# An attention and mixer kernel on one core: attention values formed in 64x64 quarters over two PSUM banks, tail transposes moved into another bank and one step later

## The chip, the cores and the metric

The kernel runs on one core of a Trainium2 chip. The metric is the device time of one execution in microseconds; the times below are medians over runs on the chip. A profile is taken of one execution, and all rows in this document come from that execution.

## What is computed

The program is an attention block with a learned relative-position bias, followed by two mixer blocks. The change touches only the attention block:

```
q, k, v: (B=4, H=8, S=576, D=64)
scores = q @ k^T / sqrt(64)
rel    = |i - j|;  x = log1p(rel) / log1p(max(i, 1))
bias   = relu(x * w1 + b1) @ w2                  # one value per head, row, column
attn   = softmax(scores + bias)
out    = attn @ v                                # (4, 8, 576, 64), all float32
...
x = first mixer(out);  result = second mixer(x)
```

576 = 4 x 128 + 64, so each head has four full row tiles of 128 and a tail of 64 rows, and likewise four full blocks of keys and a tail of 64 keys.

## The kernel before, in words

**Units.** Attention is worked through in 80 units. A unit is one batch `b`, one pair of heads `p` and one row tile `it`; `it` = 4 (`NM`) is the tail of 64 rows, whose two heads share one tile. The first 20 units are batch 0, in the order tail, 0, 1, 2, 3, with the four head pairs inside. The next 50 units are ten (batch, head pair) groups of five units in the order 0, 1, tail, 2, 3; these groups are called *paired* here (function `paired`), because the values of two row tiles are formed together. The last 10 units are two groups that are not paired.

**Steps.** The main loop (L656 of the kernel before) runs steps n = -3 to 80. Step n works on several units at once, and what it emits is the order in which each engine does it:

- PE: `scores(n+3)`: queries times keys in 64x64 quarters (`ss`, L456): lhsT is 64 rows x 64 columns of the array, and the four quarters go to two PSUM tiles, one for each half of the array's rows.
- DVE: scale, bias and row minimum (`pr`, L464), then ACT: exp with a row sum (`softmax`, L475), then POOL: division by the sum (`normalise`, L488).
- PE: `turn(n)`: the probabilities of unit n are transposed, 128x128 at a time: four blocks of keys of the first head into the bank `x` (L515), four of the second head into the bank `y` (L520), and the two heads' tail keys into the bank `z` (L521, L523). ACT copies `x` (L516) and `z` (L528, `z_out`) to SBUF, DVE copies `y` (L532, `y_out`).
- PE: `q_turn(n+5)`, in batch 0 alone: a query tile is transposed into the second half of the bank `z` (L412), and ACT copies it out (L423, L425, `q_out`).
- PE: `values`: the transposed probabilities times `v`. `values` (L542 to L547) forms one unit; `values2` (L565 to L570) forms two row tiles of a paired group in two halves, in two steps, the second half with the tail keys. The first head goes to the array's columns 0 to 63 and the second to 64 to 127 (128 rows x 64 columns, two matmuls side by side); the tail keys are 64 rows x 64 columns. All of it is summed in one bank `o`, and DVE copies it into X (`place`, L438, or L552 for the 64-row tail).

**Where the values stand.** `values` and `values2` calls come at a step's end (`late_v`: after transposes and, in batch 0, bias work), but one of each paired group comes early in a step (`early_v`: `values` of the group's tail unit, straight after `scores`). Of the 80 calls, 40 are halves of `values2` and 40 are `values`; 10 of the latter are the paired groups' early ones, and one more early one stands near the end.

**Bias.** The first 15 steps (n = -3 to 11) also make the bias: per step two groups of 16 rows. DVE makes three quarters of the hidden layer and ACT one (`hidden`, L320 and L322), PE multiplies (`bps`, L363; 32 matmul records a step) and ACT copies out (`bias_place`, L376). Steps 0 to 3 are tail units and have no `y`; from step 4 on there is one.

**PSUM.** There are eight banks. Four are `s0` and `s1` (scores and bias products, two banks each), and one each `x`, `y`, `z` and `o`. A tile of such a bank is given out again when the last reader of the tile before has ended; the wait for that stands on the first instruction that writes the new tile. The engines run in the order in which the code emits, and each waits at the head of its own queue.

Float32 matmuls stand in the trace as two records each (two passes), transposes as one.

Of the kernel before, what the change touches and what calls it, by code (L numbers as in the profile page):

```python
# [7 lines left out]
F32 = mybir.dt.float32  # L8
# [3 lines left out]
ALU = mybir.AluOpType  # L12
# [7 lines left out]
def kernel(ctx, tc, ins, consts, out, dbg=None, nb=4, stop=None):  # L20
    nc = tc.nc
    V, S, G, T, D = nc.vector, nc.scalar, nc.gpsimd, nc.tensor, nc.sync

    q, k, v = ins["q"], ins["k"], ins["v"]
    B, H, N, HD = q.shape
    P = 128
    NP = H // 2
    NM = N // P
    TL = N - NM * P
# [9 lines left out]
    ident = cpool.tile([P, P], F32, name="ident")  # L39
    X = cpool.tile([P, ND, NT], F32, name="X")  # L40
# [14 lines left out]
    halves = (slice(0, HD), slice(HD, P))  # L55
# [112 lines left out]
    units = [(0, p, it) for it in order0 for p in range(NP)]  # L168
# [5 lines left out]
    NB = N + TL  # L174
# [4 lines left out]
    bias_t = apool.tile([P, NP, N], F32, name="bias_t")  # L179
    raw_p = tc.alloc_tile_pool(name="raw", bufs=2)  # L180
    hl_p = tc.alloc_tile_pool(name="hl", bufs=2)
    pp = tc.alloc_tile_pool(name="pp", bufs=4)
    pt_p = tc.alloc_tile_pool(name="pt", bufs=1)
    sm_p = tc.alloc_tile_pool(name="sm", bufs=4)

# [221 lines left out]
    def q_turn(n, z):  # L407

        b, p, it = units[n]
        w = P if it < NM else TL  # L410
        if b == 0:
            T.transpose(z[:, 1, 0:w], qraw.pop((b, p, it)), ident[0:w, 0:w])  # L412
        else:
            queries[n] = turned(b, p)[:, it * P:it * P + w]

    def q_out(n, z):
        b, p, it = units[n]
        if b > 0:
            return
        w = P if it < NM else TL  # L420
        t = hl_p.tile([P, P], F32, tag="q0", name="q0", bufs=5)[:, 0:w]
        if it < NM:
            S.copy(out=rows(t), in_=dealt(z[:, 1]))  # L423
        else:
            S.copy(out=t, in_=z[:, 1, 0:w])  # L425
        queries[n] = t


# [1 line left out]
    def dealt(x):  # L430
        return x.rearrange("p (t j s) -> p t s j", j=GT, s=P // GT)

    def rows(x):
        return x.rearrange("p (t s j) -> p t s j", j=GT, s=P // GT)

    def place(p, c0, o):

        V.tensor_copy(  # L438
            out=X[:, p, c0:c0 + o.shape[1]].rearrange("p (t j s) -> p t j s", j=GT, s=P // GT),
            in_=o.rearrange("p (t s j) -> p t j s", j=GT, s=P // GT),  # L440
        )
# [62 lines left out]
    def room(n):  # L504
        if not paired(n):
            return rooms[0], n % 2
        it = units[n][2]
        return (rooms[0], it) if it < 2 else (rooms[1], 1 if it == NM else it - 2)

    def turn(n, pr, z):  # L510
        b, p, it = units[n]
        (xs, ys, zs), s_ = room(n)
# [4 lines left out]
        if it < NM:  # L517
            y = ps_t.tile([P, NM, P], F32, tag="y", name="y")
            for t in range(NM):
                T.transpose(y[:, t], pr[:, NB + t * P:NB + (t + 1) * P], ident)  # L520
            T.transpose(z[:, 0], pr[:, NM * P:N + TL], ident)  # L521
            return ys[:, s_], zs[:, s_], y
        T.transpose(z[0:TL, 0], pr[:, NM * P:N], ident)  # L523
        return None, zs[:, s_], None

    def z_out(z, zs, y):
        r = slice(0, P if y is not None else TL)
        S.copy(out=zs[r], in_=z[r, 0])  # L528
# [5 lines left out]
    def values(n):  # L534
        b, p, it = units[n]
        vm, vt = vraw[b, p]
        (xs, ys, zs), s_ = room(n)
        xs, ys, zs = xs[:, s_], ys[:, s_], zs[:, s_]
        o = ps_t.tile([P, P], F32, tag="o", name="o")
        w = P if it < NM else TL  # L540
        for t in range(NM):
            T.matmul(o[0:HD, 0:w], lhsT=vm[:, t, 0], rhs=xs[:, t, 0:w], start=t == 0, stop=False)  # L542
            rh = ys[:, t] if it < NM else xs[:, t, TL:P]
            T.matmul(o[HD:P, 0:w], lhsT=vm[:, t, 1], rhs=rh, start=t == 0, stop=False)
        T.matmul(o[0:HD, 0:w], lhsT=vt[0:TL, 0], rhs=zs[0:TL, 0:w], start=False, stop=True)
        lh, rh = (vt[TL:P, 1], zs[TL:P]) if it < NM else (vt[0:TL, 1], zs[0:TL, TL:P])
        T.matmul(o[HD:P, 0:w], lhsT=lh, rhs=rh, start=False, stop=True)  # L547
        c0 = b * N + it * P
        if it < NM:
            place(p, c0, o)  # L550
        else:
            V.tensor_copy(out=X[:, p, c0:c0 + w], in_=o[:, 0:w])  # L552

    open_o = []

    def values2(n, half):

        b, p, it = units[n]
        vm, vt = vraw[b, p]
        xs, ys, zs = room(n)[0]  # L560
        if half == 0:
            open_o.append(ps_t.tile([P, 2 * P], F32, tag="o", name="o"))
        o = open_o[0]
        for t in range(2 * half, 2 * half + 2):
# [4 lines left out]
        T.matmul(o[0:HD], lhsT=vt[0:TL, 0], rhs=zs[0:TL], start=False, stop=True)
        T.matmul(o[HD:P], lhsT=vt[TL:P, 1], rhs=zs[TL:P], start=False, stop=True)  # L570
        c0 = b * N + it * P
        place(p, c0, open_o.pop())
# [32 lines left out]
    for gi in range(GUP):  # L605
        if gi == NQ:
            load_q0(order0[1])
        if gi < NP:
            k_parts0(gi, hl_p if gi < 2 else first, "" if gi < 2 else "x")
        if HP and gi > 0:  # L610
            bias_place(groups[gi - 1], bps)
        if gi == TW:
            times_w1(slice(TC, 2 * N))
        if gi >= 1:
            hide(gi + 2)
        if not HP and gi > 0:
            bias_place(groups[gi - 1], bps)
        bps = bias_product(gi, hs.pop(gi))
        if gi >= GUP - 2:
            u = gi - (GUP - 2)  # L620
            z = ps_t.tile([P, 2, P], F32, tag="z", name="z")
            q_turn(u, z)
            q_out(u, z)
    bias_place(groups[GUP - 1], bps)
# [33 lines left out]
    st = {}  # L658
    for n in range(-3, U + 1):
# [7 lines left out]
            normalise(*st[n + 2])  # L667
        if len(gs) > 0:
            hide(gs[0] + 2)
        z = ps_t.tile([P, 2, P], F32, tag="z", name="z") if n < U else None  # L670
        form(early_v.pop(n, []))
        if n == U - 1:
            early_x([NM])
        if 0 <= n < U:
            ys, zs, y = turn(n, st[n][0], z)
        if n == U - 3:

            flat = bias_m.rearrange("p i h n -> p (i h n)").bitcast(F32R)
# [8 lines left out]
        if 0 <= n + 5 < U:  # L687
            q_turn(n + 5, z)
# [3 lines left out]
        if 0 <= n < U:  # L692
            z_out(z, zs, y)
        if 0 <= n + 5 < U:
            q_out(n + 5, z)
# [654 lines left out]
```

## Time and profile before

| what | us |
|---|---|
| median of 3 runs | 914.84 (914.71 to 916.07) |
| the profiled execution, its time | 913.72 |
| its span, first to last instruction | 911.9 |
| PE busy | 894.5 (98%) |
| DVE busy | 625.6 (69%) |
| ACT busy | 394.0 (43%) |
| POOL busy | 293.7 (32%) |
| granted TensorE clock, mean | 0.997 of 2.4 GHz |

Attention takes about the first 340 us. A timeline row gives the start in us from the span's start, the duration in us, engine, line, operation, tiles (out<-in), for PE the array's rows*columns, shapes (partitions x elements) and the number of instructions merged in the row; in square brackets stands how long the engine had been idle and what ended that. PE is its matmuls, PEld its weight loads. Ends of matmuls are modelled, so on PE the starts are what to read.

### The profile page before, as it was taken

How to read it: one execution, taken by the hardware profiler on the slowest of the kernel's cores; microseconds unless marked ns; L12 is line 12 of the kernel's file. 1: busy time of each engine (PE TensorE's matmuls, PEld its weight loads, DVE VectorE, ACT ScalarE, POOL GpSimd, SP SyncE). 2: the span in 40 equal slices, each digit the busy share in tenths (PEclk: the TensorE clock that was granted, in tenths of full speed). 3: DMA queues.
4: the chain of work that ended last, by engine and by line, in shares of the span. 5: the costliest groups of instructions: out<-in, count | busy, mean ns of one | idle time of the engine just before them, and what ended most of it. 6: DMA issues, size and time to landing. Idle time of an engine off the chain costs nothing.

```text
span 911.9 us, 18151 instructions
## 1 busy us (share of the span) xinstructions
PE 894.5 (98%) x7018; PEld 749.8 (82%) x7018; DVE 625.6 (69%) x1371; ACT 394.0 (43%) x875; POOL 293.7 (32%) x430
## 2 busy tenths in 40 slices
PE   8799999999999999999999999999999999999998
PEld 3366776665666789899999999999999989889996
DVE  6799777887877769988834343232215999896756
ACT  6799766676666754433312121211114532222310
POOL 2366455555545532233310100100002452423230
PEclk9999999999999999999999999999999999999999
DMA  8775534333332113223400100000041001010002
GB/s 157 161 155 118 115 64 94 54 66 68 56 64 56 29 60 93 94 93 121 133 24 24 38 33 24 24 24 1 1 77 48 24 1 47 1 59 1 1 13 92
DMA packets 118966, 54.87 MB, mean 60 GB/s; under 512 B 100832, under 2 KB 107616, under 8 KB 118880
## 3 DMA queue, kind: packets, MB, share of 16 engines
q1 hardware_dynamic: 118880, 53.72, 24.7%
q8 instruction: 55, 0.90, 0.4%
q14 instruction: 31, 0.25, 0.1%
HBM read 38.36 MB, written 4.72 MB: 47 GB/s over the span
## 4 chain that ended last, share of the span: by engine, by line
PE 78%; DVE 16%; issue 2%; ACT 2%; DMA 2%; SPq 0%; DVEq 0%; ACTq 0%
PE a L985 14%; PE pg L822 14%; PE ss L456 9%; PE x L515 5%; PE o L565 4%; PE po L1202 4%; PE pv L1096 4%; PE ps L1171 4%; PE o L542 3%; PE y L520 3%; PE bps L363 3%; PE pu L1149 3%; DVE res L940 2%; DVE w L131 2%; PE pu L854 1%
## 5 line engine op out<-in xcount | busy, mean ns | idle before, releaser
L488 POOL TENSOR_SCALAR pr<-pr,sm 128x576 f32<-128x576 f32 (+2 forms) x208 | 129.1, 637 | 118.8 <-DVE sm L482 114.2
L985 PE MATMUL a<-g,c 128*128 128x384 f32 x864 | 162.4, 335 | 1.8 <-DVE X L993 1.0
L985 PEld LDWEIGHTS a<-g,c 128*128 128x128 f32 x864 | 150.9, 188 | 3.5 <-ACT g L828 2.2
L829 DVE SCALAR_TENSOR_TENSOR g<-pg,g 128x384 fp32r<-128x384 f32 x72 | 40.0, 556 | 163.7 <-ACT g L828 163.7
L822 PE MATMUL pg<-u,c 128*128 128x384 f32 x720 | 134.5, 334 | 0.0
L822 PEld LDWEIGHTS pg<-u,c 128*128 128x128 f32 x720 | 125.6, 188 | 0.1
L828 ACT ACTIVATE g<-pg 128x384 fp32r<-128x384 f32 x72 | 35.3, 490 | 192.2 <-PE pg L822 192.2
L475 ACT ACTIVATE pr<-pr,mn 128x576 f32<-128x576 f32 x144 | 112.0, 778 | 6.9 <-DVE mn L464 6.0
L464 DVE CUSTOM_DVE_ANT_0 pr<-ss,bias_m 128x576 f32<-128x576 f32 x128 | 91.3, 750 | 29.8 <-PE ss L456 29.2
L456 PE MATMUL ss<-kt,X 64*64 64x288 f32 x864 | 77.1, 412 | 0.0
L940 DVE STREAM_TRANSPOSE res<-X 32x256 f32<-32x256 f32 (+1 forms) x176 | 68.1, 387 | 2.8
L60 POOL TENSOR_TENSOR c<-w,c 128x512 fp32r<-128x512 f32 x24 | 35.5, 1479 | 88.9 <-ACT c L59 78.7
L60 POOL TENSOR_TENSOR wi<-w,wi 128x512 fp32r<-128x512 f32 x8 | 14.0, 1754 | 153.0 <-DVE g L829 112.5
L320 DVE TENSOR_SCALAR X<-ttab,wsm 128x576 f32<-128x576 f32 x108 | 62.3, 639 | 0.0
L515 PEld LDWEIGHTS x<-ident,pr 128*128 128x128 f32 x320 | 33.6, 141 | 30.4 <-POOL pr L488 18.9
L1171 PE MATMUL ps<-wsT,vn 128*128 128x288 f32 x384 | 56.5, 296 | 1.1 <-DVE tmp L1181 1.1
L456 PEld LDWEIGHTS ss<-kt,X 64*64 64x64 f32 x864 | 36.6, 132 | 22.3 <-DVE sm L482 7.3
L1171 PEld LDWEIGHTS ps<-wsT,vn 128*128 128x128 f32 x384 | 52.7, 189 | 1.9 <-DVE tmp L1181 1.8
L120 ACT ACTIVATE sq<-wraw 128x512 f32<-128x512 f32 (+2 forms) x43 | 27.9, 648 | 57.5 <-DVE w L136 56.3
L515 PE MATMUL x<-ident,pr 128*128 128x128 f32 x320 | 52.5, 286 | 0.0
L1149 PEld LDWEIGHTS pu<-y,wi 128*128 128x128 f32 x384 | 51.4, 188 | 0.3
L1149 PE MATMUL pu<-y,wi 128*128 128x288 f32 x384 | 51.6, 295 | 0.0
(188 smaller groups left out, 1760.0 us busy)
## 6 DMA issues: line engine op xcount, KB each, us to landing
wraw<-in_moe_w_ch_dram SPq DMA_DIRECT2D x24, 512.0 KB, 3.5
bias_m<-bst SPq DMA_DIRECT2D x32, 288.0 KB, 3.7
vm<-in_v_dram SPq DMA_DIRECT2D x32, 128.0 KB, 2.8
wraw<-in_moe_w_in_dram SPq DMA_DIRECT2D x8, 512.0 KB, 3.4
out_dram<-res SPq DMA_DIRECT2D x16, 256.0 KB, 2.0
kr<-in_k_dram SPq DMA_DIRECT2D x48, 72.0 KB, 2.4
qr<-in_q_dram SPq DMA_DIRECT2D x48, 72.0 KB, 2.4
wraw<-in_moe_w_out_dram SPq DMA_DIRECT2D x4, 512.0 KB, 3.6
```

The lines of the kernel that those rows point to most:

```text
L60: (eng or V).tensor_tensor(out=lo, in0=src, in1=hi.bitcast(F32), op=ALU.subtract)
L320: V.tensor_scalar(out=hd, in0=tt, scalar1=b1i, scalar2=None, op0=ALU.min)
L456: T.matmul(ss[a % na][o, hf, 0:HN], lhsT=qt[r, m * HD:(m + 1) * HD], rhs=kt[r, js], start=True, stop=True)
L464: V.tensor_tensor_reduce(out=pr[:, a * NB:a * NB + N].rearrange("p (f n) -> p f n", f=2), in0=ss[a][:, :, 0:HN], in1=bias[a].rearrange("p ...
L475: S.activation(out=pr[:, a * NB:a * NB + N], in_=pr[:, a * NB:a * NB + N], func=AF.Exp, scale=-1.0, bias=mn[:, a:a + 1], accum_out=sm[:, a ...
L488: G.tensor_scalar(out=pr[:, dc:dc + hi - lo], in0=pr[:, lo:hi], scalar1=sm[:, a:a + 1], scalar2=1.0, op0=ALU.mult, op1=ALU.mult,)
L515: T.transpose(x[:, t], pr[:, t * P:(t + 1) * P], ident)
L822: T.matmul(pg, lhsT=c1[f][i][:, d], rhs=u[j][:, d], start=d == 0 and n == 0, stop=d == ND - 1 and n == 2)
L940: V.transpose(out=o, in_=src(c)[32 * a:32 * a + 32])
L985: T.matmul(acc[d], lhsT=c2[f][i][:, d * P:(d + 1) * P], rhs=g[j], start=f == f0 and n == 0, stop=f == f1 and n == 2,)
L1149: T.matmul(pu[:, hf, 0:HN], lhsT=wi[i][:, d, f * P:(f + 1) * P], rhs=y[j][:, d, js], start=d == 0 and m == 0, stop=d == ND - 1 and m == 2,)
L1171: T.matmul(ps[:, hf, 0:HN], lhsT=vn[i][:, t, ds_], rhs=wsT[j][:, t, js], start=t == 0 and m == 0, stop=False,)
```

## The change

Four things change, all in attention.

1. **Quarters.** `values` and `values2` split each 128-row matmul into two of 64 rows. The upper half of the rows is summed in the bank `o`, the lower half in the bank that was `z`; a call now takes both banks. All values matmuls, like the tail keys and the scores, are 64 rows x 64 columns. There are twice as many records for the full key blocks (960 more), of the same lengths.
2. **Placing.** `place` first lets ACT copy the second bank into X (L442), then DVE adds the first bank to it (L443), instead of one copy by DVE.
3. **Tail keys.** The bank `z` being taken, the transposes of tail keys (`turn_tail`) and of queries (`q_turn`) go into a tile `zq` of the bank `y`. Tail keys of unit n are transposed in step n+1, at the start of the step's transposes, and copied out by ACT (`z_out`, `q_out`) ahead of the copy of `x`. The four `y` transposes then need that bank back.
4. **Buffers.** Since tail keys are read one step later, `pp` (probabilities) has five buffers for four.

```diff
-    pp = tc.alloc_tile_pool(name="pp", bufs=4)
+    pp = tc.alloc_tile_pool(name="pp", bufs=5)
...
-    def place(p, c0, o):
-
-        V.tensor_copy(
-            out=X[:, p, c0:c0 + o.shape[1]].rearrange("p (t j s) -> p t j s", j=GT, s=P // GT),
-            in_=o.rearrange("p (t s j) -> p t j s", j=GT, s=P // GT),
-        )
+    def place(p, c0, os, w):
+
+        out, (a, b) = X[:, p, c0:c0 + w], [o[:, 0:w] for o in os]
+        if w >= P:
+            out = out.rearrange("p (t j s) -> p t j s", j=GT, s=P // GT)
+            a, b = [t.rearrange("p (t s j) -> p t j s", j=GT, s=P // GT) for t in (a, b)]
+        S.copy(out=out, in_=b)
+        V.tensor_tensor(out=out, in0=a, in1=out, op=ALU.add)
...
+    def turn_tail(n, pr, z):
+
+        if units[n][2] < NM:
+            T.transpose(z, pr[:, NM * P:N + TL], ident)
+        else:
+            T.transpose(z[0:TL], pr[:, NM * P:N], ident)
...
-        o = ps_t.tile([P, P], F32, tag="o", name="o")
+        os = [ps_t.tile([P, 2 * P], F32, tag=t, name="o") for t in "oz"]
         for t in range(NM):
-            T.matmul(o[0:HD, 0:w], lhsT=vm[:, t, 0], rhs=xs[:, t, 0:w], start=t == 0, stop=False)
             rh = ys[:, t] if it < NM else xs[:, t, TL:P]
-            T.matmul(o[HD:P, 0:w], lhsT=vm[:, t, 1], rhs=rh, start=t == 0, stop=False)
...
+            for o, r in zip(os, halves):
+                T.matmul(o[0:HD, 0:w], lhsT=vm[r, t, 0], rhs=xs[r, t, 0:w], start=t == 0, stop=t == NM - 1 and o is os[1])
+                T.matmul(
+                    o[HD:P, 0:w], lhsT=vm[r, t, 1], rhs=rh[r], start=t == 0,
+                    stop=t == NM - 1 and (o is os[0]) == (it < NM),
+                )
...
-        z = ps_t.tile([P, 2, P], F32, tag="z", name="z") if n < U else None
         form(early_v.pop(n, []))
         if n == U - 1:
             early_x([NM])
+        zq = ps_t.tile([P, 2, P], F32, tag="y", name="zq") if n < U else None
+
+        tails = [l for l in ([n - 1] if n < U - 2 else {U - 2: [n - 1, n], U - 1: [n], U: []}[n]) if l >= 0]
+        for i, l in enumerate(tails):
+            turn_tail(l, st[l][0], zq[:, i])
+        if 0 <= n + 5 < U:
+            q_turn(n + 5, zq[:, 1])
+        for i, l in enumerate(tails):
+            z_out(l, zq[:, i])
+        if 0 <= n + 5 < U:
+            q_out(n + 5, zq[:, 1])
         if 0 <= n < U:
-            ys, zs, y = turn(n, st[n][0], z)
+            ys, y = turn(n, st[n][0])
```

How the order moves, at two places. The first is PE in a step of a paired group whose values are a first half of `values2`. `ss` are scores, `x`, `y`, `z` and `zq` the transposes, `o` the values; behind each row stand the engines whose semaphores it waits for. Before:

```order
L456 MATMUL ss<-kt,X 64x288 [waits DVE_49]
L456 MATMUL ss<-kt,X 64x288 x7
L515 MATMUL x<-ident,pr 128x128 [waits Activation_49,Pool_49]
L515 MATMUL x<-ident,pr 128x128 x3
L520 MATMUL y<-ident,pr 128x128 [waits DVE_49,Pool_49]
L520 MATMUL y<-ident,pr 128x128 x3
L521 MATMUL z<-ident,pr 128x128 [waits Activation_49]
L565 MATMUL o<-rb,vm 64x256
L566 MATMUL o<-rb,vm 64x256
```

and with the change:

```order
L458 MATMUL ss<-kt,X 64x288 [waits DVE_49]
L458 MATMUL ss<-kt,X 64x288 x7
L515 MATMUL zq<-ident,pr 128x128 [waits DVE_49]
L529 MATMUL x<-ident,pr 128x128 [waits Activation_49,Pool_49]
L529 MATMUL x<-ident,pr 128x128 x3
L535 MATMUL y<-ident,pr 128x128 [waits Activation_49,Pool_49]
L535 MATMUL y<-ident,pr 128x128 x3
L574 MATMUL o<-rb,vm 64x256
L575 MATMUL o<-rb,vm 64x256
```

The tail transpose moved from behind `y` to ahead of `x`, and the first `y` transpose now waits for ACT (the copy out of `zq`, which lies in the same bank) as well as for POOL.

The second place is ACT in a bias step, from one step's second `bias_place` (L376) through the next step's copy of `x`. `zA` and `q` are what `z_out` and `q_out` write. Before:

```order
L376 ACTIVATE bst<-bps,evb 128x576 [waits DMAHW2_49,PE_49]
L475 ACTIVATE pr,sm<-pr,mn 128x576 [waits DVE_49]
L322 ACTIVATE X<-ttab,wsm 128x576 [waits Activation_49] x2
L516 COPY xA<-x 128x512 [waits PE_49]
L475 ACTIVATE pr,sm<-pr,mn 128x576 [waits DVE_49,Pool_49]
L528 COPY zA<-z 128x128 [waits PE_49]
L423 COPY q_1280<-z 128x128
```

and with the change:

```order
L376 ACTIVATE bst<-bps,evb 128x576 [waits DMAHW2_49,PE_49]
L477 ACTIVATE pr,sm<-pr,mn 128x576 [waits DVE_49]
L322 ACTIVATE X<-ttab,wsm 128x576 [waits Activation_49]
L442 COPY X<-o 128x128 [waits PE_49]
L322 ACTIVATE X<-ttab,wsm 128x576 [waits Activation_49]
L522 COPY zA<-zq 128x128 [waits PE_49]
L423 COPY q_1328<-zq 128x128
```

The copies of tail keys and queries moved ahead of the copy of `x` and of an exp, behind both hidden-layer pieces (L322), and the placing copy (L442) is new between those two.

## Rows read from the trace of the kernel before

**Rows 1.** The page, part 1: busy us (share of the span), instructions.

```profile
PE 894.5 (98%) x7018; PEld 749.8 (82%) x7018; DVE 625.6 (69%) x1371; ACT 394.0 (43%) x875; POOL 293.7 (32%) x430
```

**Rows 2.** Busy time by stretch: bias steps (60 to 104 us), paired groups (137 to 301).

```profile
core 0: us, PE busy (x) PEld busy (x) DVE busy (x) ACT busy (x) POOL busy (x), PEclk, DMA share, GB/s
60.00:104.00 44.00, 43.86 (x612) 29.16 (x614) 41.36 (x98) 39.73 (x85) 27.31 (x45) 1.00 0.57 127
...
137.00:301.00 164.00, 164.00 (x1702) 100.38 (x1701) 126.64 (x341) 108.39 (x283) 87.43 (x181) 1.00 0.33 63
```

**Rows 3.** Timeline, PE, one step of a paired group (first half of `values2`).

```profile
182.70 0.60 PE L520 MATMUL y<-ident,pr 128*128 128x128 f32 x4
183.14 0.27 PE L521 MATMUL z<-ident,pr 128*128 128x128 f32 x1
183.34 0.43 PE L565 MATMUL o<-rb,vm 128*64 128x256 f32 x1
...
183.60 0.38 PE L565 MATMUL o<-rb,vm 128*64 128x256 f32 x1
...
184.04 0.38 PE L565 MATMUL o<-rb,vm 128*64 128x256 f32 x1
...
184.35 1.20 PE L456 MATMUL ss<-kt,X 64*64 64x288 f32 x16
185.48 0.66 PE L515 MATMUL x<-ident,pr 128*128 128x128 f32 x4
```

**Rows 4.** Timeline, PE, the early `values` of a paired group's tail unit.

```profile
195.71 0.27 PE L542 MATMUL o<-rb,vm 128*64 128x64 f32 x1
...
195.82 0.22 PE L542 MATMUL o<-rb,vm 128*64 128x64 f32 x1
...
195.88 0.22 PE L542 MATMUL o<-rb,vm 128*64 128x64 f32 x1
...
196.59 0.33 PE L515 MATMUL x<-ident,pr 128*128 128x128 f32 x1
```

**Rows 5.** Timeline, ACT and DVE, just ahead of those early values.

```profile
194.79 0.20 ACT L475 ACTIVATION_READ_ACCUMULATOR pr<-pr,mn 128x1 f32 x1
...
194.89 0.42 DVE L438 COPY X<-o 128x256 f32<-128x256 f32 x1
```

**Rows 6.** Timeline, ACT, copy of the `x` that ended just ahead of rows 3.

```profile
182.90 0.58 ACT L516 COPY xA<-x 128x512 f32<-128x512 f32 x1 [0.70 <-PE x L515]
```

**Rows 7.** Timeline, restarts of PE after a wait for DVE's minimum.

```profile
26.14 0.08 DVE L464 DVE_READ_ACCUMULATOR2_ANT mn<- 128x1 f32 x1
...
26.27 0.70 PE L363 MATMUL bps<-X,yA 128*32 128x288 f32 x2 [4.56 <-DVE mn L464]
...
43.95 0.08 DVE L464 DVE_READ_ACCUMULATOR2_ANT mn<- 128x1 f32 x1
...
44.18 0.47 PE L363 MATMUL bps<-X,w2q 128*32 128x288 f32 x4 [0.36 <-DVE mn L464]
```

**Rows 8.** Timeline, PE, one bias step from `y` to the next `y`.

```profile
88.04 0.60 PE L520 MATMUL y<-ident,pr 128*128 128x128 f32 x4
...
88.79 2.19 PE L363 MATMUL bps<-X,w2q 128*32 128x288 f32 x32
...
93.76 0.60 PE L520 MATMUL y<-ident,pr 128*128 128x128 f32 x4
```

**Rows 9.** Timeline, ACT, the same bias step.

```profile
89.50 0.25 ACT L528 COPY zA<-z 128x128 f32<-128x128 f32 x1
89.64 0.28 ACT L423 COPY q<-z 128x128 f32<-128x128 f32 x1
...
91.06 0.74 ACT L376 ACTIVATE bst<-bps,evb 128x576 f32<-128x576 f32 x1
...
92.45 1.43 ACT L322 ACTIVATE X<-ttab,wsm 128x576 f32<-128x576 f32 x2
```

**Rows 10.** Timeline, ACT and DVE, end of an earlier bias step without `y`.

```profile
53.78 0.77 ACT L322 ACTIVATE X<-ttab,wsm 128x576 f32<-128x576 f32 x1
...
53.85 0.21 DVE L552 COPY X<-o 128x64 f32<-128x64 f32 x1
```

More of the change, by code (lines that the diff above doesn't have):

```diff
@@ L411, in q_turn @@
         if b == 0:
-            T.transpose(z[:, 1, 0:w], qraw.pop((b, p, it)), ident[0:w, 0:w])
+            T.transpose(z[:, 0:w], qraw.pop((b, p, it)), ident[0:w, 0:w])
         else:
@@ L422, in q_out @@
         if it < NM:
-            S.copy(out=rows(t), in_=dealt(z[:, 1]))
+            S.copy(out=rows(t), in_=dealt(z))
         else:
-            S.copy(out=t, in_=z[:, 1, 0:w])
+            S.copy(out=t, in_=z[:, 0:w])
         queries[n] = t
@@ L508, in room, with z_out, turn @@
         return (rooms[0], it) if it < 2 else (rooms[1], 1 if it == NM else it - 2)
-    def turn(n, pr, z):
+    def turn_tail(n, pr, z):
[3 more added lines that the diff above has]
+            T.transpose(z[0:TL], pr[:, NM * P:N], ident)
+    def z_out(n, z):
+        r = slice(0, P if units[n][2] < NM else TL)
+        (_, _, zs), s_ = room(n)
+        S.copy(out=zs[r, s_], in_=z[r])
+    def turn(n, pr):
         b, p, it = units[n]
-        (xs, ys, zs), s_ = room(n)
+        (xs, ys, _), s_ = room(n)
         x = ps_t.tile([P, NM, P], F32, tag="x", name="x")
@@ L516, in turn @@
         S.copy(out=xs[:, s_], in_=x)
[L517 to L528, printed above, removed]
+        if it == NM:
+            return None, None
+        y = ps_t.tile([P, NM, P], F32, tag="y", name="y")
+        for t in range(NM):
+            T.transpose(y[:, t], pr[:, NB + t * P:NB + (t + 1) * P], ident)
+        return ys[:, s_], y
     def y_out(ys, y):
@@ L538, in values @@
         xs, ys, zs = xs[:, s_], ys[:, s_], zs[:, s_]
-        o = ps_t.tile([P, P], F32, tag="o", name="o")
         w = P if it < NM else TL
+        os = [ps_t.tile([P, 2 * P], F32, tag=t, name="o") for t in "oz"]
         for t in range(NM):
-            T.matmul(o[0:HD, 0:w], lhsT=vm[:, t, 0], rhs=xs[:, t, 0:w], start=t == 0, stop=False)
             rh = ys[:, t] if it < NM else xs[:, t, TL:P]
-            T.matmul(o[HD:P, 0:w], lhsT=vm[:, t, 1], rhs=rh, start=t == 0, stop=False)
-        T.matmul(o[0:HD, 0:w], lhsT=vt[0:TL, 0], rhs=zs[0:TL, 0:w], start=False, stop=True)
-        lh, rh = (vt[TL:P, 1], zs[TL:P]) if it < NM else (vt[0:TL, 1], zs[0:TL, TL:P])
-        T.matmul(o[HD:P, 0:w], lhsT=lh, rhs=rh, start=False, stop=True)
[L548 to L552, printed above, removed]
+            for o, r in zip(os, halves):
[4 more added lines that the diff above has]
+                )
+        T.matmul(os[0][0:HD, 0:w], lhsT=vt[0:TL, 0], rhs=zs[0:TL, 0:w], start=False, stop=True)
+        o, lh, rh = (os[1], vt[TL:P, 1], zs[TL:P]) if it < NM else (os[0], vt[0:TL, 1], zs[0:TL, TL:P])
+        T.matmul(o[HD:P, 0:w], lhsT=lh, rhs=rh, start=False, stop=True)
+        place(p, b * N + it * P, os, w)
     open_o = []
@@ L561, in values2 @@
         if half == 0:
-            open_o.append(ps_t.tile([P, 2 * P], F32, tag="o", name="o"))
-        o = open_o[0]
+            open_o.append([ps_t.tile([P, 2 * P], F32, tag=t, name="o") for t in "oz"])
+        os = open_o[0]
         for t in range(2 * half, 2 * half + 2):
-            T.matmul(o[0:HD], lhsT=vm[:, t, 0], rhs=xs[:, :, t], start=t == 0, stop=False)
-            T.matmul(o[HD:P], lhsT=vm[:, t, 1], rhs=ys[:, :, t], start=t == 0, stop=False)
+            for o, r in zip(os, halves):
+                T.matmul(o[0:HD], lhsT=vm[r, t, 0], rhs=xs[r, :, t], start=t == 0, stop=t == NM - 1 and o is os[1])
+                T.matmul(o[HD:P], lhsT=vm[r, t, 1], rhs=ys[r, :, t], start=t == 0, stop=t == NM - 1 and o is os[0])
         if half == 0:
             return
[L569 to L572, printed above, removed]
+        T.matmul(os[0][0:HD], lhsT=vt[0:TL, 0], rhs=zs[0:TL], start=False, stop=True)
+        T.matmul(os[1][HD:P], lhsT=vt[TL:P, 1], rhs=zs[TL:P], start=False, stop=True)
+        place(p, b * N + it * P, open_o.pop(), 2 * P)
     early_v, late_v = {}, {}
@@ L620 @@
             u = gi - (GUP - 2)
-            z = ps_t.tile([P, 2, P], F32, tag="z", name="z")
+            z = ps_t.tile([P, P], F32, tag="y", name="zq")
             q_turn(u, z)
@@ L691 @@
             softmax(*st[n + 3], which=(0,))
[L692 to L695, printed above, removed]
         if gs:
```

2 lines of the change are left out of this document (removed).

## The prediction

> **What bounds the kernel now.** The page's busy times come first: PE is busy 98% of the span, DVE 69%, ACT 43% [rows 1]. Those are averages, so the table by stretch comes next. In the bias steps PE is full, but DVE is busy 41.4 of 44 us and ACT 39.7, so three engines are near their limit; in the paired groups ACT is busy 108 of 164 us and PE alone is full [rows 2]. The last view is the timeline, since a busy PE still loses time between matmuls. Equal transposes start 0.11 us apart (183.14 less 182.70, over four), but the first values matmul starts 0.20 after the last transpose: 0.09 is lost where PE goes from 128x128 to 128x64. Passes then follow each other in 0.22 (183.60 to 184.04 is two), but the first took 0.26. From the last pass, 184.04 + 0.22 = 184.26, to the scores at 184.35 another 0.09 is lost [rows 3]. So a change of array shape costs **0.09 to drain and 0.05 to refill, 0.14 us**. That is what this change can win.
>
> **What it removes.** The passes themselves keep their length: the scores already run four quarters side by side, sixteen records in 1.13 us, four at a time about 0.25 with the drain taken off [rows 3], so a pass of 256 columns in four quarters should take the same 0.22 as in two halves. Switches go: one in each of 20 first halves of `values2` (values to scores), one in each of 20 second halves and 29 late `values` (full blocks to tail keys), two in each of 11 early `values`. That is 91, times 0.14 = 12.7 us. Not all are paid out. The 10 late calls in bias steps lie in a stage that ACT will pace (below), and the 20 of the paired groups' early calls and of the step before them are swallowed by a new wait (below). 61 x 0.14 = **8.5 us** remain as gain.
>
> **The y transposes wait for ACT.** This is the first new wait. `zq` lies in the bank `y`, so `y` starts only after ACT has copied `zq`, and behind it on PE stand the values and the next scores. Count from the start of the `zq` transpose. As first of its stretch it lasts 0.33 [rows 4]. ACT takes up a finished transpose about 0.03 later: the last `x` starts 0.11 ahead of `y`, at 182.59, lasts 0.27, and its copy starts at 182.90 [rows 3, 6]. ACT had been idle 0.70 us then, so the copy of `zq` starts at once, at 0.36, lasts 0.25 [rows 9] and ends at 0.61. How long PE needs to start again has two prices in the trace: 0.05 in one case (26.14 + 0.08 to 26.27), 0.15 in the other (44.03 to 44.18) [rows 7]. In the built order the `bps` of the second case waits for two engines, DVE and POOL, and it is the first-named that comes last. The changed `y` waits for ACT and POOL, the same pattern, so I take 0.15; 0.05 is the other end. So `y` starts at 0.76 (or 0.66). Left alone it would start at 0.61: five spacings of 0.11, and 0.06 because a first transpose is 0.33 long, not 0.27 [rows 3, 4]. The stall is 0.15, and after it the weights are not preloaded, another 0.06: **0.21 us a step**, with 0.11 as lower end. There are 64 `y`; 7 lie in the bias cycle and 10 are covered by the next wait. 47 x 0.21 = **9.9 us**. (In steps 11 to 14 a query copy is added behind; by 0.05 or 0.15 for the restart that makes 0.17 or 0.27, and I leave them at 0.21.)
>
> **Early values wait for two evacuations in a row.** Both banks must be free: ACT's copy, then DVE's add. Before, these values started at 195.71, limited by PE, and DVE's copy ran from 194.89 to 195.31. Now ACT is free for the copy 0.09 after 194.79, at 194.88 [rows 5]; PE's tail keys end about then, since the removed switch (-0.14) and the stalled `y` (+0.21) nearly cancel, say 194.91. A copy of 256 columns lies between 0.25 for 128 and 0.58 for 512 [rows 6, 9], by length 0.36: 195.27. With 0.05 to pass on, DVE's add at the 0.42 of its copy [rows 5], and 0.05 to restart PE, values start at 195.79. That is 0.08 later than before, ten times: **0.8 us**. The other placings end ahead of DVE's next row minimum and cost PE nothing; DVE's add takes the place of a copy of equal length. If ACT were late there, the add would hold up the row minimum behind it and the scores' banks; ACT's one third of idle time is the cover.
>
> The Trainium skill, page "TensorEngine Tiling (Array Packing)", section "PSUM Bottleneck", says that tiling speeds up TensorE but not the emptying of PSUM, which may then become the bottleneck. The bias steps agree, and ACT's 66% in the paired groups does not; by the rule the two late placings of each paired group would hold PE too, a rival below.
>
> **The bias steps get a cycle through ACT.** Follow one from `y` to `y`. Four `y` at 0.11, drain 0.09 and refill 0.06 make 0.59 to the first `bps`. The second `bias_place` starts 2.27 after it (88.79 to 91.06), limited by PE, and the hidden-layer pieces 1.39 later (92.45) [rows 8, 9]. In the new order there follow on ACT: one L322 at 0.67 (two take 1.43), the placing copy at 0.16 (such copies follow each other in 0.14), the second L322 at 0.67, `z_out` at 0.14, `q_out` to its end at 0.28 [rows 9], and 0.05 for PE. The sum is **6.22 us**, against 5.72 now (88.04 to 93.76). Before, nothing on PE waited for that chain. The cycle needs `y` and both L322 pieces, so it runs into steps 4 to 10: 7 x 0.50 = 3.5 us. In steps 1 to 3 DVE sets the pace. There the placing copy takes the start of the second L322, 53.78, lasts about the 0.21 of DVE's copy, and with 0.05 the add starts at 54.04 rather than 53.85 [rows 10]: 3 x 0.2 = 0.6. Together **4.1 us**.
>
> The fifth `pp` buffer costs nothing: tail keys are read a step later from one buffer more. No DMA is added, and SP's and POOL's orders keep their places.
>
> **The sum.** 9.9 + 0.8 + 4.1 - 8.5 = +6.3 us. Against the profiled execution, 913.72, this gives 920.0; the median of the runs shown stands 1.1 higher, 914.84, and the forecast for it is **921.1 us**. With 0.11 for each `y`, the sum is 5.2 + 0.5 + 4.1 - 8.5 = +1.3, or 916.1. On the other side a placing copy that holds ACT for its whole length (0.28, not 0.16) adds 0.8, and an early start 0.3 later, as if DVE were also busy then, adds 3: 925. What can be told from no change is about 0.2%, 1.8 us.
>
> **Rivals.**
> - *Faster: `y` does not wait.* If the copy of `zq` is released before PE reaches `y`, only 4.1 - 8.5 = -4.4 is left: 910.4. It decides at a stall of (8.5 - 4.1 - 0.5) / 47 = 0.083 us a `y`. For it: four `x` lie between, ACT is idle ahead of them, and the release misses by only hundredths. Against it: restart and refill alone, by their lower ends, make 0.11.
> - *The bias cycle does not close*, because ACT gets ahead somewhere. The 4.1 go and the 10 switches there still gain nothing, DVE being 94% busy [rows 2]: 917.0. For it: ACT's chain is long and I may have counted a piece that overlaps. Against it: the order shows every piece between `bps` and `y`.
> - *Short passes cost by their number.* In 16 `values` of tail units (4, 10 and 2) a pass moves 64 columns and takes 0.06 for two matmuls [rows 4]; if four took twice that, 16 x 8 x 0.06 = 7.7 come on top: 928.8. The scores' four at once speak against it. The Trainium skill, same page, section "Instruction Overhead", says that every matmul carries some 60 cycles and that a tiling factor should not be taken out of a dimension that is already small.
> - *Evacuation ends last in the paired groups too.* 20 late placings at 0.36 + 0.05 add 8.2: 929.3. ACT's idle time speaks against it.
> - *The quarters do not run side by side.* The 160 passes of `values2` alone would add 160 x 0.22 = 35 us: above 950. Rows 3 speak against it.
>
> **How the numbers follow.** Chances: forecast 0.57, `y` does not wait 0.17, no bias cycle 0.13, short passes 0.05, evacuation 0.03, no quarters 0.02, something unthought of 0.03. The forecast's own range is 916.1 to 925. The 8-in-10 range reaches down to 911.0, through the third case and the upper part of the second, and up to 926.0. Left out are most of the three slow rivals and the lower half of the fast one, about 0.2. Faster takes nearly all of the `y` case: 0.17. Same takes half of the no-cycle case and the forecast's lower edge: 0.13. Slower has the rest: 0.70.
>
> **What would show it.** Right: no 0.09 gap between values, tail keys and scores; a gap of about 0.15 between the fourth `x` and the first `y` in paired groups, and PE's `y` named as waiting for ACT; 6.2 us from `y` to `y` in bias steps; early values starting behind DVE's add. Wrong: `y` following `x` at 0.11 (then it is faster), bias steps still at 5.7, a 256-column pass in four quarters that takes more than 0.22, or DVE's row minima waiting for ACT in paired groups.

## The result and the profile after

The changed kernel takes **925.0 us** (median of four runs, 923.81 to 925.59) against 914.78 of the kernel before in the same session (914.29 to 916.07): a ratio of 1.0106, 95% interval 1.0093 to 1.0118. It is slower by about 10 us; the forecast was 921.1 with a range of 911.0 to 926.0. The profiled execution took 925.59, the longest of the four, with a span of 923.8; against the profiled one of before (span 911.9) that is 11.9 more, 1.7 more than the medians differ. The sums below are made on these two traces.

The page's busy times, and then the two stretches of the table by stage (us, PE, PEld, DVE, ACT, POOL busy, PEclk, DMA), which answer to [rows 1, 2]:

```profile
PE 898.6 (97%) x7978; PEld 758.6 (82%) x7978; DVE 626.7 (68%) x1371; ACT 414.8 (45%) x935; POOL 294.4 (32%) x430
```

```profile
60.00:104.00 44.00, 40.88 (x685) 27.20 (x686) 40.88 (x93) 37.52 (x85) 28.00 (x45) 1.00 0.52 115
137.00:301.00 164.00, 163.01 (x2171) 106.27 (x2170) 123.98 (x335) 120.06 (x305) 85.02 (x177) 1.00 0.35 67
```

In the bias steps no engine is full any more: PE fell from 43.86 to 40.88 of 44 us, and DVE and ACT are less busy too. A chain that passes from one to another sets the pace there. In the paired groups PE still fills its time and ACT went from 108 to 120.

The timeline of PE in a step of a paired group (columns: start, duration, engine, line, operation and tiles), answering to [rows 3]:

```profile
194.18 0.33 PE L515 MATMUL zq<-ident,pr 128*128 128x128 f32 x1
194.34 0.60 PE L529 MATMUL x<-ident,pr 128*128 128x128 f32 x4
194.95 0.63 PE L535 MATMUL y<-ident,pr 128*128 128x128 f32 x4
...
196.22 0.38 PE L574 MATMUL o<-rb,vm 64*64 64x256 f32 x1
...
196.43 0.38 PE L578 MATMUL o<-rb,vt 64*64 64x256 f32 x1
196.44 0.45 PE L458 MATMUL ss<-kt,X 64*64 64x288 f32 x2
```

and ACT's copy in the same step:

```profile
194.54 0.27 ACT L522 COPY zA<-zq 128x128 f32<-128x128 f32 x1 [0.64 <-PE zq L515]
```

The pass of 256 columns in four quarters takes 0.21 (196.22 to 196.43), and tail keys and scores follow without the 0.09 of [rows 3]: that is the gain. The loss stands two rows higher. Four `x` at 0.11 end at 194.78, and `y` starts at 194.95, 0.14 after ACT's copy ended at 194.81. So `y` waits for the copy of `zq`, 0.17 here, and its first transpose is 0.03 longer. (The row names no engine that ended a wait, because `x` is modelled to end only 0.01 ahead of `y`.)

The bias steps, PE and then ACT, answering to [rows 8, 9]:

```profile
88.20 0.66 PE L535 MATMUL y<-ident,pr 128*128 128x128 f32 x4 [0.42 <-ACT q L423]
88.78 2.19 PE L363 MATMUL bps<-X,w2q 128*32 128x288 f32 x32
...
94.41 0.66 PE L535 MATMUL y<-ident,pr 128*128 128x128 f32 x4 [0.42 <-ACT q L423]
```

```profile
92.44 0.76 ACT L322 ACTIVATE X<-ttab,wsm 128x576 f32<-128x576 f32 x1
93.11 0.25 ACT L442 COPY X<-o 128x128 f32<-128x128 f32 x1
93.26 0.78 ACT L322 ACTIVATE X<-ttab,wsm 128x576 f32<-128x576 f32 x1
93.93 0.26 ACT L522 COPY zA<-zq 128x128 f32<-128x128 f32 x1
94.08 0.28 ACT L423 COPY q<-zq 128x128 f32<-128x128 f32 x1
```

From `y` to `y` it is 6.21 us, 5.72 before; ACT's chain is the one that the prediction counted, piece by piece, and it is what PE waits for (`<-ACT q L423`).

Where `y` waits longer than in the paired groups: a step that also turns queries, and the third last unit.

```profile
119.43 0.60 PE L529 MATMUL x<-ident,pr 128*128 128x128 f32 x4
120.22 0.63 PE L535 MATMUL y<-ident,pr 128*128 128x128 f32 x4 [0.19 <-issue]
...
333.51 0.60 PE L529 MATMUL x<-ident,pr 128*128 128x128 f32 x4
334.51 0.63 PE L535 MATMUL y<-ident,pr 128*128 128x128 f32 x4 [0.39 <-POOL pr L490]
```

ACT in these two steps:

```profile
119.68 0.27 ACT L522 COPY zA<-zq 128x128 f32<-128x128 f32 x1 [1.13 <-PE zq L412]
119.84 0.27 ACT L423 COPY q<-zq 128x128 f32<-128x128 f32 x1
...
333.75 0.46 ACT L120 ACTIVATE sq<-wraw 128x288 f32<-128x288 f32 x1
334.11 0.25 ACT L522 COPY zA<-zq 128x128 f32<-128x128 f32 x1
```

`x` takes 0.44 to hand over; here `y` starts 0.79 and 1.00 after it, so 0.35 and 0.56 are lost. In the first, the copy of the tail keys waited for the query transpose too (`<-PE zq L412`), since both write one tile, and the query copy follows. In the second, `zq` was over at 333.68, but ACT still had the end of a placing copy and the squaring of a piece of the token weights (L120) ahead of its copy, which started at 334.11. The trace names POOL there, but `zA` ended at 334.36 and `y` started 0.15 later, as elsewhere.

**Where the 11.9 us lie.** The starts of the scores in the two timelines, stage by stage; the shift of the changed kernel against before, and the prediction's terms for the same stretch:

| stretch (start of a step's scores) | before, us | shift gained, measured | by the terms |
|---|---|---|---|
| start to step 1 | 0 to 41.08 | +1.76 | 0 |
| steps 1 to 11, with bias | to 103.38 | +5.11 | 4.1 + 0.21 - 0.14 = +4.2 |
| steps 12 to 21 | to 137.60 | +1.58 | 10 x (0.21 - 0.14) = +0.7 |
| steps 22 to 71, paired groups | to 305.51 | +1.70 | 30 x 0.21 + 0.8 - 40 x 0.14 = +1.5 |
| step 72 to the first token-stage transposes | to 325.94 | +1.80 | 6 x 0.21 - 10 x 0.14 = -0.1 |
| the rest | to 911.91 | -0.05 | 0 |

### The profile page after: what moved, and what is told of

It reads as the page before. It is cut to its first block, busy times and chain, and to the rows that moved or that the text cites. A ratio compares the mean times of both kernels' runs of the same rounds, so it can differ in the third digit from the quotient of the medians.

```text
span 923.8 us, 20192 instructions
## 1 busy us (share of the span) xinstructions
PE 898.6 (97%) x7978; PEld 758.6 (82%) x7978; DVE 626.7 (68%) x1371; ACT 414.8 (45%) x935; POOL 294.4 (32%) x430
## 4 chain that ended last, share of the span: by engine, by line
PE 74%; DVE 15%; ACT 6%; issue 2%; DMA 2%; POOL 0%; SPq 0%; DVEq 0%; ACTq 0%; POOLq 0%
PE a L997 14%; PE pg L834 14%; PE ss L458 7%; PE po L1214 4%; PE o L574 4%; PE pv L1108 4%; PE y L535 4%; PE bps L363 4%; PE ps L1183 3%; PE x L529 3%; PE pu L1161 3%; PE o L552 2%; DVE res L952 2%; DVE w L131 2%; PE zq L515 2%
## 5 line engine op out<-in xcount | busy, mean ns | idle before, releaser
L320 DVE TENSOR_SCALAR X<-ttab,wsm 128x576 f32<-128x576 f32 x108 | 59.5, 614 | 0.0
L120 ACT ACTIVATE sq<-wraw 128x512 f32<-128x512 f32 (+2 forms) x43 | 27.9, 650 | 56.8 <-DVE w L136 53.0
L458 PEld LDWEIGHTS ss<-kt,X 64*64 64x64 f32 x864 | 41.7, 132 | 14.2 <-issue 1.9
L529 PE MATMUL x<-ident,pr 128*128 128x128 f32 x320 | 48.0, 273 | 0.0
L535 PE MATMUL y<-ident,pr 128*128 128x128 f32 x256 | 40.4, 281 | 6.2 <-ACT q L423 3.1
```

The source lines that it names most:

```text
L320: V.tensor_scalar(out=hd, in0=tt, scalar1=b1i, scalar2=None, op0=ALU.min)
L458: T.matmul(ss[a % na][o, hf, 0:HN], lhsT=qt[r, m * HD:(m + 1) * HD], rhs=kt[r, js], start=True, stop=True)
```

## The experiments

The theory: what the quarters win (0.14 us a switch) is real, and the new place of the tail keys loses more, by `y` waiting for ACT and by the cycle in the bias steps. The main rival: the quarters, or emptying two banks by two engines, cost the time. All ratios below are to the kernel before, timed in the same session.

**1. Only the move of the tail keys** (the values are as before the change).

```diff
-        S.copy(out=out, in_=b)
-        V.tensor_tensor(out=out, in0=a, in1=out, op=ALU.add)
...
+        V.tensor_copy(
...
+        o = ps_t.tile([P, P], F32, tag="o", name="o")
...
-        os = [ps_t.tile([P, 2 * P], F32, tag=t, name="o") for t in "oz"]
...
+            T.matmul(o[0:HD, 0:w], lhsT=vm[:, t, 0], rhs=xs[:, t, 0:w], start=t == 0, stop=False)
...
-            for o, r in zip(os, halves):
...
```

> Values as before the change (two halves, one bank, DVE's copy alone); only the tail keys stay moved: transposed one step later, in the bank of the second head, with the fifth buffer. By the prediction's terms the gain of 8.5 us is gone, and of the waits those that the move alone makes stay: 57 y at 0.21 us (47, and the 10 that the early values no longer swallow) = 12.0, and the bias cycle without the placing copy, 6.06 instead of 5.72, seven times = 2.4. That is 14.4 over the kernel before, 929 us, and the gap from the fourth x to the first y should be about 0.3 us in every step. The rival, that the quarters and their emptying by two engines are what costs and the move is nearly free, expects 915 to 918.

Measured: 930.39 us, ratio 1.0175 (1.0161 to 1.0189). Its timeline of PE, a paired step and two bias steps:

```profile
190.70 0.60 PE L527 MATMUL x<-ident,pr 128*128 128x128 f32 x4
191.36 0.63 PE L533 MATMUL y<-ident,pr 128*128 128x128 f32 x4
...
85.13 0.66 PE L533 MATMUL y<-ident,pr 128*128 128x128 f32 x4
...
91.18 0.66 PE L533 MATMUL y<-ident,pr 128*128 128x128 f32 x4
```

The bias period is 6.05, where 6.06 was expected; in the paired groups ten steps grow by 1.65 us (7.96 less 6.57 is 1.39 in the first ten, 1.65 in each later ten), 0.21 for each of eight `y`. The move alone makes the loss, and more of it than the whole change does. The rival (915 to 918) falls.

**2. Tail keys in bank z wherever it is free.**

```diff
-            z = ps_t.tile([P, P], F32, tag="y", name="zq")
+            z = ps_t.tile([P, P], F32, tag="z", name="zq")
...
-        zq = ps_t.tile([P, 2, P], F32, tag="y", name="zq") if n < U else None
+        free = n != U - 1 and (not U0 <= n < U - 2 * NS or (n - U0) % NS == 0)
+        zq = ps_t.tile([P, 2, P], F32, tag="z" if free else "y", name="zq") if n < U else None
```

> The change, but tail keys and queries go to bank z wherever no values are open in it: in the start-up, in all steps that aren't paired, and in the first step of each paired group; bank y only in the other paired steps and in the step of the last unit. By the theory of the y wait, 27 of the 47 stalls go, 27 x 0.21 = 5.7 us, and the bias cycle runs over the placing copy and the transposes instead of over z_out and q_out: 0.59 + 2.27 + 1.39 + 0.67 + 0.28 + 0.05 + 0.44 + 0.44 = 6.1 less what the queries overlap, between 5.7 and 6.1, so 1 to 3.4 us go there. Together 916 to 918.5 us, against 925.0 of the change. The rival, that quarters or their two-engine emptying made the loss, expects the time of the change within 1 us.

Measured: 916.40 us, ratio 1.0019 (1.0010 to 1.0028), within the range. Its `y` in two bias steps:

```profile
85.05 0.60 PE L535 MATMUL y<-ident,pr 128*128 128x128 f32 x4
...
90.93 0.60 PE L535 MATMUL y<-ident,pr 128*128 128x128 f32 x4
```

The bias period is 5.87 to 5.88 us, and steps 12 to 21 go from +1.58 to -1.07. One bank's name is worth 8.6 us, with quarters and both copies kept.

**3. The placing copy earlier on ACT.** Run 2, and:

```diff
-            hide(gs[1] + 2)
+            hide(gs[1] + 2, range(3))
...
         form(late_v.pop(n, []))
+        if len(gs) > 1:
+            hide(gs[1] + 2, (3,))
...
```

> As the run with tail keys in bank z, and ACT's quarter of the second hidden-layer group of a bias step is issued after the values, so that the placing copy comes 0.67 us earlier on ACT. If the bias steps of that run still wait for the placing copy, their period falls to what DVE and PE allow, about 5.7 us, and in steps 1 to 3 the 0.2 each go: 1 to 3 us below that run. If they do not wait for it, the time stays within 0.7 us of it, or gets longer, since the hidden layer comes later.

Measured: 914.93 us, ratio 0.9999 (0.9990 to 1.0009), 1.5 below run 2. Its `y` in two bias steps:

```profile
82.05 0.60 PE L535 MATMUL y<-ident,pr 128*128 128x128 f32 x4
...
87.75 0.60 PE L535 MATMUL y<-ident,pr 128*128 128x128 f32 x4
```

5.70, the pace of before: the cycle through ACT is gone.

**4. Tail keys of several units at once in the paired groups.** Run 3, and:

```diff
-    pp = tc.alloc_tile_pool(name="pp", bufs=5)
+    pp = tc.alloc_tile_pool(name="pp", bufs=6)
...
+        if U0 < n <= U - 2 * NS:
+            tails = {2: [n - 2, n - 1, n], 0: [n - 2, n - 1]}.get((n - U0) % NS, [])
...
```

> As the run with the copy earlier, and in paired groups the tail keys of several units are transposed together: three units in the group's third step, which has no y, two in the first step of the next group, in bank z; a sixth buffer keeps the probabilities that long. No y of a paired group waits for a copy of ACT any more. By the theory of the y wait that takes away the last 20 stalls (20 x 0.21 = 4.2 us) and the shift of the early values (0.8), and gives back the switches that the stalls had swallowed: 907 to 911 us, faster than before the change. By the rival that y's wait is not what costs in the paired groups (emptying by two engines, or the passes), the time stays within 1.5 us of the run with the copy earlier.

Measured: **907.95 us**, ratio 0.9928 (0.9914 to 0.9942): faster than both kernels. In its timeline the tail keys stand where no `y` follows, and `y` follows `x` after 0.50 (four spacings and a first transpose 0.06 longer):

```profile
201.35 0.44 PE L515 MATMUL zq<-ident,pr 128*128 128x128 f32 x2
201.62 0.27 PE L517 MATMUL zq<-ident,pr 128*64 128x128 f32 x1
...
204.25 0.66 PE L529 MATMUL x<-ident,pr 128*128 128x128 f32 x4
204.75 0.60 PE L535 MATMUL y<-ident,pr 128*128 128x128 f32 x4
```

The paired stretch (steps 22 to 71) now gains 5.64 us on before, where the change lost 1.70.

**5. Run 4 without the quarters**: the values of run 1 in it.

> The run with batched tails, but values formed as before the change: two halves, one bank, DVE's copy alone. It undoes the quarters in a kernel where no y of a paired group waits for ACT, so the difference of the two is what the quarters are worth. By the term of 0.14 us a switch: six switches in each of ten paired groups less the wait for both banks that the early values keep there, 0.84 - 0.27 = 0.57, 5.7 us; ten late calls in steps 12 to 22, 1.4; about 0.8 at the end of the stage; nothing in the bias steps, where PE isn't alone at its limit. Together 7.9 us above the run with batched tails, 914.5 to 916.5. The rival, that the batching or the freer banks made that run fast, expects 908 to 910.

Measured: 914.86 us, ratio 1.0004 (0.9995 to 1.0012): 6.9 above run 4. In the paired stretch the two differ by 5.87 (+0.23 and -5.64; 5.7 expected), in steps 12 to 21 by 1.31 (1.4 expected), in the bias steps by 0.4. The end stretch went against the expectation: there the quarters cost 1.15 (+0.07 and +1.22), not gained 0.8. The batching by itself wins nothing. The quarters do, in the batched kernel, though not at the end of the stage (run 8 removes two waits there).

**6. Early values behind `y`** in the paired groups, on run 4.

```diff
         for t in range(NM):
             T.transpose(x[:, t], pr[:, t * P:(t + 1) * P], ident)
...
+        form(early_v.pop(n, []))
         S.copy(out=xs[:, s_], in_=x)
...
```

> The run with batched tails, and in the paired groups the early values of the tail unit stand behind x and y of their step, ahead of the next scores, not ahead of x. By the theory that these values wait for ACT's copy and DVE's add in a row, about 0.2 to 0.27 us of PE's time goes ten times, as the transposes now cover it, and the number of switches stays: 2.0 to 2.7 us less, 905.3 to 906. The rival is that ACT's copy of x, which must now follow these values since it writes where they read, comes so late that the next step waits for the x bank: then 908 or more.

Measured: 910.73 us, ratio 0.9962 (0.9949 to 0.9976), a miss: slower than run 4, by 1.3 us in the paired stretch. The wait of the early values did go, and another came. PE, then DVE, in this run:

```profile
214.79 1.63 PE L458 MATMUL ss<-kt,X 64*64 64x288 f32 x16
```

```profile
211.94 0.22 DVE L443 TENSOR_TENSOR X<-o,X 128x64 f32<-128x64 f32 x1 [0.61 <-ACT X L442]
212.09 0.68 DVE L541 COPY rb<-y 128x512 f32<-128x512 f32 x1
212.68 1.13 DVE L726 STREAM_TRANSPOSE X<-qr 128x512 f32<-128x512 f32 x1
...
213.78 0.71 DVE L466 CUSTOM_DVE_ANT_0 pr<-ss,bias_m 128x576 f32<-128x576 f32 x1
...
214.42 0.75 DVE L466 CUSTOM_DVE_ANT_0 pr<-ss,bias_m 128x576 f32<-128x576 f32 x1
```

The sixteen score matmuls take 1.63, 1.15 elsewhere. They wait for a bank that the second of DVE's row minima, at 214.42 and over at 215.17, has yet to read. It stands behind the first minimum (213.78), that behind two transposes of queries, those behind the copy of `y`, and that behind the add of the early values, ahead of which DVE now idles 0.61. The named rival (ACT's copy of `x`) was not the cause; the trace shows this chain, but no run took it apart.

**7. Tail keys in bank y at the end**, on run 6.

```diff
-        free = n != U - 1 and (not U0 <= n < U - 2 * NS or (n - U0) % NS == 0)
+        free = n < U - 3 and (not U0 <= n < U - 2 * NS or (n - U0) % NS == 0)
```

> The run with the early values behind y, and in the last three units of the attention part the tail keys stand in bank y again, since there PE waited 0.65 us, instead of 0.20 of a plain switch, for bank z in two steps that have no scores to cover the values' copies. By the theory each of these two waits turns into a y stall of about 0.26: 0.3 to 0.5 us less in all, to be seen in the trace of these steps, hardly in the median. The rival, that these waits are not for the bank, expects them unchanged and the y stalls on top, 0.5 us more.

Measured: 909.76 us, ratio 0.9955 (0.9943 to 0.9968); the end stretch is 0.57 longer than in run 6 (+1.79 and +1.22): a miss, by about what the rival gave. Bank z was what those two steps had waited for, since the gaps ahead of `zq` fell from 0.65 and 0.63 to 0.38 and 0.20; but a `y` that waits there costs more than 0.26, 0.81 in this one (1.25 less 0.44), since ACT has the same squaring (L120) ahead of the copy of `zq`:

```profile
317.24 0.60 PE L529 MATMUL x<-ident,pr 128*128 128x128 f32 x4
318.49 0.63 PE L534 MATMUL y<-ident,pr 128*128 128x128 f32 x4 [0.65 <-ACT zA L522]
```

The median is 1.0 below that of run 6, but in the profiles this lies ahead of the paired groups and behind the attention block, in stretches that the edit does not touch.

**8. At the end in a bank of the scores**, on run 4.

```diff
+        if n in (U - 3, U - 2):
+            zq = s_tile("zq")[:, :, 0:P]
```

> The run with batched tails, and in the two steps behind the last scores the tail keys stand in one of the scores' banks, which are free by then, so that they wait neither for the values' copies (bank z) nor hold y (bank y). By the theory both waits of 0.65 us fall to the 0.20 of a plain switch, 0.9 us less: about 907.0. If PE waited there for something other than the bank, the gaps stay and the time is that of the run with batched tails, 908, within 0.3.

Measured: 907.61 us, ratio 0.9918 (0.9905 to 0.9932). PE at the last unit but one, first in run 4, then here:

```profile
317.45 0.27 PE L559 MATMUL o<-zA,vt 64*64 64x128 f32 x1
318.08 0.44 PE L515 MATMUL zq<-ident,pr 128*128 128x128 f32 x2 [0.36 <-ACT X L442]
```

```profile
319.30 0.27 PE L559 MATMUL o<-zA,vt 64*64 64x128 f32 x1
319.50 0.44 PE L515 MATMUL zq<-ident,pr 128*128 128x128 f32 x2
```

Both waits fell to 0.20, and the end stretch by 0.88 (+1.22 to +0.34), as expected; in the median no more than 0.3 shows.

**9. The change once more**, for its start-up.

> The changed kernel itself, once more. In its profile the start-up and the first step were 1.8 us behind the kernel before, though the run that only moves the tail keys, with the same instructions up to there, was 0.6 behind. If that was chance, this profile shows the second scores within 0.8 us of before, and the time comes out between 924 and 925.6; if the quarters cost something there, it is 1.8 again.

Measured: 925.41 us, ratio 1.0112 (1.0098 to 1.0126). Step 1 again came late, by 2.20. But chance can do as much: run 8 stood at +1.63 and run 4 at -0.45 with the same instructions up to there. One difference between those two profiles is DVE's scaling of the table, here in run 4 and in run 8, each with POOL's first products:

```profile
4.33 0.63 DVE L290 TENSOR_SCALAR ttab<-ttab,wsm 128x704 f32<-128x704 f32 x1 [1.02 <-DMA ttab<-const_tab_dram]
...
4.63 2.46 POOL L341 TENSOR_TENSOR yA<-w2b,wsm 128x512 f32<-128x512 f32 x2
```

```profile
4.62 3.23 DVE L290 TENSOR_SCALAR ttab<-ttab,wsm 128x704 f32<-128x704 f32 x1 [1.24 <-DMA ttab<-const_tab_dram]
...
4.70 2.04 POOL L341 TENSOR_TENSOR yA<-w2b,wsm 128x512 f32<-128x512 f32 x2
```

**10 and 11. POOL held behind that scaling**, in the change and in run 8.

```diff
+    seen = first.tile([P, 1], F32, name="seen")
+    G.tensor_copy(out=seen, in_=ttab[:, 0:1])
```

> The changed kernel, and POOL's first two-input products (L341) are held behind DVE's first scaling of the table (L290) by a copy of one column of that table on POOL. In the profiles so far L290 takes 0.6 us where it starts 0.24 us or more ahead of those products and 3.0 to 3.3 where it starts later, and the start-up of a run is late where it took 3. By this theory L290 takes 0.6 us here, the second scores come 0.2 to 0.9 us behind the kernel before instead of 1.8 and 2.2, and the median falls by 0.5 to 1.5, to 923.5 to 925. If the quarters or the bank of the queries made the start-up late, the second scores stay 1.8 us behind and the time stays at 925 to 925.5.

> The run with the end in the scores' banks, and POOL's first products held behind L290 in the same way. By the theory the slow start-up, which that run's profile had (L290 3.23 us, second scores 1.6 behind the kernel before), cannot happen any more: L290 0.6 us, the second scores between 0.5 ahead and 0.9 behind, the runs within a smaller spread than 906.5 to 908.9, median 906.2 to 907.2. If the order of those two makes no difference, 907.6 again with the same spread.

Measured: the change with it (run 10) 923.89 us, ratio 1.0105 (1.0091 to 1.0119); run 8 with it (run 11) 907.15 (905.95 to 907.55), ratio 0.9919 (0.9907 to 0.9932). The scaling took 0.68 and 0.61 us. In run 11 step 1 came 0.88 late, where run 8 had 1.63, within what was expected. Yet step 1 of the change still came 1.55 late, where 0.2 to 0.9 was expected, and neither ratio moved. So the scaling is short where POOL is held behind it, and its length alone is not what makes the start-up of the change late.

## Why the prediction was right

The direction and the mechanism were right, and the time of 925.0 lies within the range; the sum was 3.9 us short of the median. By its steps:

- **A switch is worth 0.14 us.** Right. Runs 4 and 5 differ by 5.87 us over the paired stretch. With about 0.21 that the early values still wait in each group of run 4 (an estimate: its last tail-unit score matmul is followed after 0.455, and 0.24 is a pass), 8.0 us for 60 switches is 0.13 each.
- **`y` waits for ACT, 0.21 us.** Right in the paired groups: 0.17 and 0.03 by the rows above in three of a group's four `y`, 0.23 and 0.03 in the fourth, and 0.21 by run 1. PE did need 0.14 after ACT's copy to start, the upper of the two prices of [rows 7], and in the bias steps 0.05, the lower, as in the prediction's two sums; the last section says what tells the two apart. Taking 0.21 for all 47 was the term that was mis-sized. It is 0.36 to 0.38 in steps 11 to 14 (the query transposes and copies, which the prediction saw at 0.27 at most and left at 0.21), 0.26 in the other unpaired steps (ACT takes up `zq` 0.09 after its transpose and not 0.03: 126.61 + 0.33 to 127.03), and up to 0.56 and 0.03 in the last ten, where ACT was not idle. This is the 0.9 missing in steps 12 to 21 and 1.0 of the 1.9 at the end (six stalls of 2.25 in all for 1.26). Of the rest at the end, 0.33 is two score blocks that take 1.22 and 1.27 to the next transposes and not 1.08; the remaining 0.6 is not accounted for.
- **The bias cycle.** Right to 0.01 us: 6.21 by the trace, 6.22 by the sum; 6.05 without the placing copy, 6.06 expected; gone in run 3. The stretch still came out 0.9 higher, half of it in steps 1 to 3 (+1.07 for 0.6).
- **Early values.** A paired group lost 0.19 us in the trace, by the terms 3 x 0.21 + 0.08 - 4 x 0.14 = 0.15. The wait for two engines in a row shows in the order of the rows: scores at 186.48, ACT's copy from 186.72 to 187.09, DVE's add at 187.12, the values at 187.60, 0.06 after the add's end. PE, DVE and ACT of the changed kernel:

```profile
186.48 1.15 PE L458 MATMUL ss<-kt,X 64*64 64x288 f32 x8
187.60 0.27 PE L552 MATMUL o<-rb,vm 64*64 64x64 f32 x1
...
187.71 0.22 PE L552 MATMUL o<-rb,vm 64*64 64x64 f32 x1
...
187.77 0.22 PE L552 MATMUL o<-rb,vm 64*64 64x64 f32 x1
```

```profile
187.12 0.42 DVE L443 TENSOR_TENSOR X<-o,X 128x256 f32<-128x256 f32 x1 [0.39 <-ACT X L442]
```

```profile
186.72 0.37 ACT L442 COPY X<-o 128x256 f32<-128x256 f32 x1
```

- **The start-up at nothing.** Open. Both profiles of the change and run 10 have it 1.55 to 2.20 us late, run 1 with the queries in the same bank 0.62, and run 8 with the queries in bank z 1.63. How much of it is chance, no run settled.
- **The rivals.** `y` does wait, the bias cycle does close, and the quarters run side by side. Short passes cost no more in quarters: early values of 64 columns follow each other in 0.06, four at a time (187.71 to 187.77), as they did two at a time in [rows 4]. The Trainium skill, page "TensorEngine Tiling (Array Packing)", section "Instruction Overhead", says that every matmul has some 60 cycles of overhead. Paid four times over at 2.4 GHz these would be 0.10 us, an estimate, so by the rows four that run side by side do not pay it four times. Apart from the early values, emptying does not end last in the paired groups: run 4 keeps all of it and is faster than both kernels. In the bias steps the placing copy is 0.16 of the cycle (6.21 less 6.05), and by the trace of run 6 the wait for DVE's add can reach PE where the early values are moved. The Trainium skill, same page, section "PSUM Bottleneck", says that the emptying of PSUM may become the bottleneck when tiling speeds up TensorE. The first of the two agrees with it, by these 0.16 us; at the second no run took the chain apart.

## What to carry to other kernels

A change that wins on the busiest engine must find a bank for what it displaces. Here the win of some 8 us was real, and the first free bank put a copy of another engine between two transposes of the full one, 0.2 to 0.6 us each time. So look for a place where the copy has something to hide behind (a step without `y`, a bank that is idle in that stage, several units at once): with these the same quarters made 907.6 us. Price a wait stage by stage: the figure from one stage held there to 0.01 us and was up to 0.38 too small where the copying engine had other work.

## What was not expected of the hardware

- DVE's scaling of a table from and to SBUF (L290) is held up by POOL's two-input products (L341) where the two start close together. In nine of the thirteen profiles the scaling started 0.24 us or more ahead of them, or POOL was held, and it took 0.58 to 0.68; in four, two of the change among them, it started between 0.18 ahead and 0.15 behind, took 3.0 to 3.3 and ended 1.11 after both products. The Trainium skill, page "SBUF — State Buffer", section "SBUF: two separate sides", says that GpSimd (POOL) and DVE, the latter in a mode that uses two ports or with two inputs from SBUF, share one pair of ports, which the first to start holds for its whole instruction while the other waits. The rows agree that one waits; in three of the four it was DVE although its row starts first. Which mode the scaling ran in no run shows.
- PE's restart after a wait has two prices, and they go with where the wait that ends last stands. Ahead of a step's first `y` transpose PE has a semaphore instruction, which takes 0.05 us. In the 53 `y` of the changed kernel from unit 15 on it is that instruction that waits for ACT, while the transpose itself waits for POOL, and `y` starts 0.14 us after the end of ACT's copy. In the nine of units 4 to 12 (a unit's `y` stands in the step of its number) the transpose itself waits for ACT, and `y` starts 0.05 after (94.36 to 94.41). [rows 7] are the same two cases: at 44.18 such an instruction waited for DVE, at 26.27 the matmul itself did. No run changed this and nothing else.
